# Four array tiles at once for the scores and the triangular products of a chunked delta-rule attention

## Chip, cores and metric

One core of a Trainium2 chip runs the whole program. The metric is the device time of one execution in microseconds (us); less is better. Engines: TensorE (PE, its weight loads PEld), VectorE (DVE), ScalarE (ACT), GpSimd (POOL), and the DMA queues, fed by SyncE (SP).

## The reference

A delta-rule attention over 4 batches x 8 heads, 768 steps, head size 48, then two dense layers with a gate over 3072 tokens of 384 features:

```python
for t in range(S):                                   # S = 768, state is (B, H, 48, 48)
    y[:, :, t] = einsum('bhd,bhde->bhe', q[:, :, t], state)
    v_old = einsum('bhde,bhd->bhe', state, kt)       # kt: normed key of step t
    state = state + bt * einsum('bhd,bhe->bhde', kt, vt - v_old)
x = y as (3072, 384)
x = maximum(maximum(x @ w1, x @ w2), x @ w3) @ w_out  # 768 wide
h = x @ w_in ; out = maximum(0.01 * h, h) @ w_out2    # 2048 wide
```

## The kernel before

The attention is worked in 12 chunks of 64 steps. A chunk's 32 pairs of batch and head are held as 16 "units" u, each with two heads: head 0 on partitions 0 to 63, head 1 on 64 to 127 (keys and queries, whose rows are the head's 48 features, lie the other way round). All attention matmuls are plain fp32, and the trace has two records, here called passes, for each of them. The dense layers use a three-matmul split in fp32r on the full 128 x 128 array (`mm3`, tiles `p` and `acc`, later `z`).

`stage2(c)` is the serial part of chunk c:

- scores and state product, tile `pk` (L240 to L250): a unit's key block is the weight (48 x 64) and [q | state] of 112 columns streams. It is done in four quarters of four units; in each, one matmul uses array rows 64 up and columns 0 to 63 (L245), the other rows 0 up and columns 64 to 127 (L246): two tiles of the array. DVE then subtracts the state part from `v` (L247, 128 x 192) and masks the scores into `W` (L214 in `masked`, twice 64 x 256).
- three triangular products in 32 x 32 blocks (`product`, L255 to L276, matmul L259), each in two halves hf of eight units: `pu` = T x v on the top 32 rows of each head, copied to `W` by ACT (L265); `pv` = GO x pu, subtracted from the low rows of `v` by DVE (L270); `pw` = T x v on the low rows, copied by ACT (L275). `pu` uses the tiles (row, column) (0,0) and (64,64), `pv` (0,32) and (64,96), `pw` (32,32) and (96,96): two tiles each.
- output `py` and state update `psu`; the output goes by DMA (`x<-st`) into the tile `x` that the first dense layer reads.

`stage1` (grams `pg`, and a solve of 31 steps on DVE, L183 and L191) prepares later pairs of chunks, and `moe1` is the first dense layer. `steps` merges these generators by weights: for chunk c, n units of dense work (9, 17, 22, then 24) are laid between the pieces of `stage2(c)` and half a `stage1`. What comes out is only a starting order: a scheduler with a timeline of its own then orders each engine's instructions, and pushes a matmul back whose PSUM buffer is not free. All small products share one ring of three PSUM buffers (tag `pa`, L82). Each engine works through its order without overtaking a waiting instruction.

Of the kernel before, what the change touches and what calls it, by code (L numbers as in the profile page):

```python
# [27 lines left out]
def kernel(  # L28
# [201 lines left out]
    def stage2(c):  # L230
# [8 lines left out]
        if c:  # L239
            for qt in range(4):  # L240
                us = slice(qt * 4, qt * 4 + 4)
                pk = pm.tile([128, 4, C + D], F32, tag="pa", name="pk")
                for j in range(4):
                    u = qt * 4 + j
                    nc.tensor.matmul(pk[0:64, j], kt[64:112, u], W[64:112, 0, u])  # L245
                    nc.tensor.matmul(pk[64:128, j], kt[0:48, u], W[0:48, 1, u])  # L246
                nc.vector.tensor_tensor(v[:, us], v[:, us], pk[:, :, cU], op=ALU.subtract)  # L247
# [7 lines left out]
        def product(name, hf, rows, outs, lhs, rhs):  # L255
            p = pm.tile([128, 8, C], F32, tag="pa", name=name)
            for j in range(8):
                for (s2, r), (_, o) in zip(rows, outs):
                    nc.tensor.matmul(p[o, j, 0:D], lhs[r, par, hf * 8 + j], rhs(s2, r, hf * 8 + j))  # L259
            return p  # L260

        for hf in range(2):
            p = product("pu", hf, tops, tops, T, lambda s2, r, u: v[r, u])
            for s2, r in tops:
                nc.scalar.activation(W[r, s2, hs[hf], cU], p[r, :, 0:D], AF.Copy)  # L265
            yield YU
        for hf in range(2):
            p = product("pv", hf, tops, lows, GO, lambda s2, r, u: W[r, s2, u, cU])
# [2 lines left out]
            yield YU
        for hf in range(2):
            p = product("pw", hf, lows, lows, T, lambda s2, r, u: v[r, u])
            for s2, r in lows:
                nc.scalar.activation(W[r, s2, hs[hf], cU], p[r, :, 0:D], AF.Copy)  # L275
            yield YU  # L276
# [379 lines left out]
```

## Time and profile before

| | us |
|---|---|
| median of 3 runs (lowest, highest) | 974.67 (974.33, 975.55) |
| profiled execution, device time | 976.32 |
| its span, first to last instruction | 974.5 |
| PE busy | 911.3 |
| DVE busy | 630.2 |
| ACT busy | 360.1 |

The span falls into a start (to 75.9 us, chunk 0 and the first solve), chunks 1 to 11 mixed with the first dense layer (75.9 to about 513), and the rest of the dense layers (to the end), in which no attention is left. Matmul ends are modelled and overlap, so the cadence of matmuls is read from the starts of rows, not from their durations.

### The profile page before, as it was taken

The numbers are of one execution on the slowest core, as the hardware profiler recorded it, in microseconds if no ns is written. First come the engines' busy times: TensorE is split into PE (matmuls) and PEld (weight loads), VectorE is DVE, ScalarE is ACT, GpSimd is POOL, SyncE is SP. The second block draws the span as 40 slices with busy tenths as digits, with TensorE's granted clock in tenths as the row PEclk, the third lists the DMA queues.
The fourth block names the chain that finished last, engine by engine and source line by source line (L and its number), as shares of the span: only waits on it lengthen the run. The fifth ranks groups of instructions, "written<-read, shape, count | busy, mean of one in ns | idle before, by whom it ended". The sixth has DMA issues, their size and how long they took to land.

```text
span 974.5 us, 19985 instructions
## 1 busy us (share of the span) xinstructions
PE 911.3 (94%) x8417; PEld 744.2 (76%) x8417; DVE 630.2 (65%) x1314; ACT 360.1 (37%) x702; POOL 12.8 (1%) x15
## 2 busy tenths in 40 slices
PE   5158999899989999999999999999999999999998
PEld 4157887678778877887877888888888888888886
DVE  4999988984984896598345836734753574444443
ACT  5432256324233232421324426635432342232332
POOL 3000000000000000000000000000000000000000
PEclk7555999999999999999999999999999999999999
DMA  9124334221250322303016504300300010000111
GB/s 258 65 90 147 107 115 123 80 60 34 75 139 18 91 83 58 76 27 85 1 35 202 170 1 146 114 1 4 126 1 1 1 49 1 0 1 33 44 54 65
DMA packets 56344, 67.83 MB, mean 70 GB/s; under 512 B 26048, under 2 KB 40000, under 8 KB 56256
## 3 DMA queue, kind: packets, MB, share of 16 engines
q1 hardware_dynamic: 56256, 66.57, 23.2%
q8 instruction: 66, 1.08, 0.5%
q14 instruction: 22, 0.18, 0.1%
HBM read 47.68 MB, written 9.44 MB: 59 GB/s over the span
## 4 chain that ended last, share of the span: by engine, by line
PE 78%; DVE 11%; DMA 4%; SPq 3%; issue 2%; ACT 1%; DVEq 0%; ACTq 0%
PE acc L331 9%; PE acc L333 9%; PE acc L332 9%; PE p L331 7%; PE z L333 7%; PE z L332 7%; PE z L331 7%; PE p L332 7%; PE p L333 6%; DVE X L191 2%; DVE tmp L183 2%; PE pv L259 2%; PE pw L259 2%; PE pk L245 2%; PE pu L259 1%
## 5 line engine op out<-in xcount | busy, mean ns | idle before, releaser
L331 PE MATMUL p<-x,w1s 128*128 128x512 f32 (+1 forms) x351 | 140.3, 400 | 10.7 <-DMA x<-st 7.6
L429 DVE TENSOR_TENSOR g<-z,g 128x512 f32<-128x512 f32 x96 | 66.1, 689 | 107.3 <-ACT g L428 107.2
L332 PE MATMUL p<-x,w1s 128*128 128x512 f32 (+1 forms) x351 | 135.2, 385 | 0.0
L333 PE MATMUL p<-x,w1s 128*128 128x512 f32 (+1 forms) x351 | 134.7, 384 | 0.0
L428 ACT ACTIVATE g<-z 128x512 f32<-128x512 f32 x96 | 57.2, 597 | 155.4 <-PE z L333 155.3
L332 PE MATMUL acc<-gs,w2g 128*128 128x512 f32 x288 | 113.5, 394 | 0.0
L333 PE MATMUL z<-x,w2g 128*128 128x512 f32 x288 | 113.3, 394 | 0.0
L333 PE MATMUL acc<-gs,w2g 128*128 128x512 f32 x288 | 113.3, 393 | 0.0
L332 PE MATMUL z<-x,w2g 128*128 128x512 f32 x288 | 113.3, 393 | 0.0
L331 PE MATMUL z<-x,w2g 128*128 128x512 f32 x288 | 113.3, 393 | 0.0
L331 PE MATMUL acc<-gs,w2g 128*128 128x512 f32 x288 | 109.7, 394 | 0.0
L48 DVE TENSOR_TENSOR gs<-g,gs 128x512 fp32r<-128x512 f32 x96 | 66.2, 689 | 40.5 <-ACT gs L47 39.1
L365 DVE TENSOR_TENSOR a<-p,a 128x512 f32<-128x512 f32 (+1 forms) x78 | 50.5, 647 | 61.5 <-PE p L333 46.5
L331 PEld LDWEIGHTS p<-x,w1s 128*128 128x128 f32 x351 | 67.9, 193 | 28.6 <-DMA x<-st 7.3
L47 ACT ACTIVATE gs<-g 128x512 fp32r<-128x512 f32 x96 | 60.4, 631 | 64.0 <-DVE g L429 63.7
L333 PEld LDWEIGHTS p<-x,w1s 128*128 128x128 f32 x351 | 68.2, 194 | 12.3
L332 PEld LDWEIGHTS p<-x,w1s 128*128 128x128 f32 x351 | 68.3, 195 | 11.3
L191 DVE TENSOR_TENSOR X<-X,tmp 128x31 f32<-128x31 f32 (+15 forms) x186 | 63.4, 341 | 5.1
L183 DVE TENSOR_TENSOR tmp<-A,X 128x31 f32<-128x31 f32 (+15 forms) x186 | 63.4, 341 | 5.0
L47 ACT ACTIVATE h<-a 128x512 fp32r<-128x512 f32 (+1 forms) x37 | 22.5, 608 | 114.6 <-DVE a L365 114.3
L331 PEld LDWEIGHTS z<-x,w2g 128*128 128x128 f32 x288 | 54.2, 188 | 12.6
L331 PEld LDWEIGHTS acc<-gs,w2g 128*128 128x128 f32 x288 | 54.1, 188 | 12.6
(107 smaller groups left out, 1627.3 us busy)
## 6 DMA issues: line engine op xcount, KB each, us to landing
x<-st SPq DMA_DIRECT2D x72, 96.0 KB, 2.5
kt<-ktr SPq DMA_DIRECT2D x12, 512.0 KB, 3.4
cv<-wi SPq DMA_DIRECT2D x16, 384.0 KB, 3.8
cv<-wo SPq DMA_DIRECT2D x16, 384.0 KB, 3.1
rx<-w SPq DMA_DIRECT2D x15, 384.0 KB, 5.6
v<-vro SPq DMA_DIRECT2D x12, 384.0 KB, 3.4
x_scratch<-xo SPq DMA_DIRECT2D x18, 256.0 KB, 2.5
xr<-x_scratch SPq DMA_DIRECT2D x12, 384.0 KB, 3.8
```

Source lines behind the costliest of these rows:

```text
L47: nc.scalar.activation(hi, src, AF.Copy)
L48: eng.tensor_tensor(lo, src, hi.bitcast(F32), op=ALU.subtract)
L183: eng.tensor_tensor(tv, A[:, k : k + 1, k + 1 : 32].to_broadcast([128, w, m]), X[:, a : a + w, k : k + 1].to_broadcast([128, w, m]), op=AL ...
L191: eng.tensor_tensor(X[:, a : a + w, k + 1 : 32], X[:, a : a + w, k + 1 : 32], tv, op=ALU.subtract)
L245: nc.tensor.matmul(pk[0:64, j], kt[64:112, u], W[64:112, 0, u])
L259: nc.tensor.matmul(p[o, j, 0:D], lhs[r, par, hf * 8 + j], rhs(s2, r, hf * 8 + j))
L331: nc.tensor.matmul(ps, whi, xhi, start=first, stop=False)
L332: nc.tensor.matmul(ps, whi, xlo, start=False, stop=False)
L333: nc.tensor.matmul(ps, wlo, xhi, start=False, stop=last)
L365: nc.vector.tensor_tensor(a, p, a, op=ALU.max)
L428: nc.scalar.activation(gg, z, AF.Copy, scale=0.01)
L429: nc.vector.tensor_tensor(gg, z, gg, op=ALU.max)
```

## The change

Quarters of `pk` are taken in pairs: for each unit of the first quarter and its fellow of the second, four matmuls on four tiles, the second quarter's two heads exchanged in the output's partitions (head 0 on 64 to 127). Its subtraction then takes two DVE instructions of 64 partitions in place of one of 128, and `masked` reads from the other half. Of the products, half 0 of `pv` and half 1 of `pu` are issued in turn (tiles in columns 0, 32, 64 and 96), and half 0 of `pw` and half 1 of `pv`; `pu` half 0 and `pw` half 1 stand alone. The dense units for chunks 2 and 3 go from 17 and 22 to 15 and 18.

```diff
-    def masked(W, i, us, p):
-        r = slice(64 * i, 64 * i + 64)
+    def masked(W, i, us, p, e=0):
+        r, o = (slice(64 * n, 64 * n + 64) for n in (i, i ^ e))
...
-        nc.vector.tensor_tensor(W[r, i, us, cP], p[r], mk, op=ALU.mult)
+        nc.vector.tensor_tensor(W[r, i, us, cP], p[o], mk, op=ALU.mult)
...
-            for qt in range(4):
+            for qt in range(0, 4, 2):
+                pk = [pm.tile([128, 4, C + D], F32, tag="pa", name="pk") for _ in range(2)]
+                for j in range(4):
+                    for e in range(2):
+                        u = (qt + e) * 4 + j
+                        o = [slice(64 * (i ^ e), 64 * (i ^ e) + 64) for i in range(2)]
+                        nc.tensor.matmul(pk[e][o[0], j], kt[64:112, u], W[64:112, 0, u])
+                        nc.tensor.matmul(pk[e][o[1], j], kt[0:48, u], W[0:48, 1, u])
                 us = slice(qt * 4, qt * 4 + 4)
...
+                nc.vector.tensor_tensor(v[:, us], v[:, us], pk[0][:, :, cU], op=ALU.subtract)
                 for i in range(2):
...
+                    masked(W, i, us, pk[0][:, :, cP])
+                us = slice(qt * 4 + 4, qt * 4 + 8)
+                for i in range(2):
+                    r, o = slice(64 * i, 64 * i + 64), slice(64 - 64 * i, 128 - 64 * i)
+                    nc.vector.tensor_tensor(v[r, us], v[r, us], pk[1][o, :, cU], op=ALU.subtract)
+                    masked(W, i, us, pk[1][:, :, cP], 1)
+                yield 2 * 970
...
+        def products(*gs):
+            ps = [pm.tile([128, 8, C], F32, tag="pa", name=g[0]) for g in gs]
             for j in range(8):
+                for p, (_, hf, rows, outs, lhs, rhs) in zip(ps, gs):
+                    for (s2, r), (_, o) in zip(rows, outs):
+                        u = hf * 8 + j
+                        nc.tensor.matmul(p[o, j, 0:D], lhs[r, par, u], rhs(s2, r, u))
+            return ps
...
+        keep(0, tops, products(pu(0))[0])
+        yield YU
+        p = products(pv(0), pu(1))
+        less(0, p[0])
+        keep(1, tops, p[1])
+        yield 2 * YU
+        p = products(pw(0), pv(1))
+        less(1, p[1])
+        keep(0, lows, p[0])
+        yield 2 * YU
+        keep(1, lows, products(pw(1))[0])
...
-            n = {1: 9, 2: 17, 3: 22}.get(c, 24)
+            n = {1: 9, 2: 15, 3: 18}.get(c, 24)
```

(`keep` is the ACT copy of L265 and L275, `less` the DVE subtraction of L270.) What the scheduler makes of it on PE, at three places:

PE, the products of chunk 11, before (`pu`, `pv`: 32 x 32 products; `p`: dense matmuls):

```order
L259 MATMUL pu<-v_5397,Tc 32x48 x16
L333 MATMUL p<-x,w1s 128x512
L331 MATMUL p<-x,w1s 128x512
L259 MATMUL pu<-v_5397,Tc 32x48 x16
L259 MATMUL pv<-W_70,GO 32x48
```

PE, the same place in the changed program, from the first `pv` on:

```order
L270 MATMUL pv<-W_70,GO 32x48
L270 MATMUL pu<-v_5380,Tc 32x48
L270 MATMUL pv<-W_70,GO 32x48
L270 MATMUL pu<-v_5380,Tc 32x48
L270 MATMUL pv<-W_70,GO 32x48 x2
L270 MATMUL pu<-v_5380,Tc 32x48 x2
L270 MATMUL pv<-W_70,GO 32x48 x2
L270 MATMUL pu<-v_5380,Tc 32x48 x2
```

The two halves, which stood one after the other, now stand two by two in turn. In chunks 1 to 11 all 11 pairs `pv`/`pu` stand so; of the pairs `pw`/`pv` those of chunks 2, 4, and 6 to 11, while in chunks 1, 3 and 5 they stand wholly or mostly in blocks.

PE, scores of chunk 3 before (the number after `pk_` tells the PSUM buffer of a quarter):

```order
L245 MATMUL pk_1886<-W1_70,kt3_281 64x112
L246 MATMUL pk_1886<-W1_70,kt3_281 64x112
L245 MATMUL pk_1916<-W1_70,kt3_281 64x112
L246 MATMUL pk_1916<-W1_70,kt3_281 64x112
L245 MATMUL pk_1916<-W1_70,kt3_281 64x112
```

PE, in the changed program, chunk 3 (`pk_1879` is the first quarter of a pair, `pk_1880` its fellow):

```order
L247 MATMUL pk_1879<-W1_70,kt3_281 64x112
L248 MATMUL pk_1879<-W1_70,kt3_281 64x112
L247 MATMUL pk_1880<-W1_70,kt3_281 64x112
L248 MATMUL pk_1880<-W1_70,kt3_281 64x112
L247 MATMUL pk_1879<-W1_70,kt3_281 64x112
L248 MATMUL pk_1879<-W1_70,kt3_281 64x112
```

PE, in the changed program, chunk 4, the same two quarters:

```order
L247 MATMUL pk_2323<-W0_69,kt4_1234 64x112
L248 MATMUL pk_2323<-W0_69,kt4_1234 64x112
L247 MATMUL pk_2323<-W0_69,kt4_1234 64x112
L248 MATMUL pk_2323<-W0_69,kt4_1234 64x112
L247 MATMUL pk_2324<-W0_69,kt4_1234 64x112
L248 MATMUL pk_2324<-W0_69,kt4_1234 64x112
```

In chunk 3 the two quarters alternate as the code has them. In chunk 4 all eight matmuls of one quarter stand ahead of the other's eight. Over the kernel the full alternation is there for one pair of quarters in each of chunks 1, 3, 5, 7, 9 and 11 (6 of 22 pairs, in some with a few matmuls in blocks); at 8 other places a quarter follows directly behind one on the other two tiles; the rest have dense work or grams between.

PE, from the second half of the products to `py` in chunk 5, before (`acc`: dense matmuls):

```order
L331 MATMUL acc_2702<-h,wo1s 128x512
L259 MATMUL pw<-v_2347,Tc 32x48 x16
L332 MATMUL acc_2700<-h,wo1s 128x512
L333 MATMUL acc_2700<-h,wo1s 128x512
L332 MATMUL acc_2701<-h,wo1s 128x512
L333 MATMUL acc_2701<-h,wo1s 128x512
L332 MATMUL acc_2702<-h,wo1s 128x512
L333 MATMUL acc_2702<-h,wo1s 128x512
L259 MATMUL pw<-v_2347,Tc 32x48 x16
L287 MATMUL py<-W_70 64x64
```

and changed:

```order
L270 MATMUL pv<-W_70,GO 32x48 x2
L270 MATMUL pu<-v_2318,Tc 32x48 x2
L270 MATMUL pw<-v_2318,Tc 32x48
L270 MATMUL pv<-W_70,GO 32x48 x16
L270 MATMUL pw<-v_2318,Tc 32x48 x31
L312 MATMUL py<-W_70 64x64
```

Here no dense matmul is left between the steps. Between the `pk` of chunk 5 and that of chunk 6 stand 22 dense matmuls in place of 63, and in chunk 4 194 in place of 153. To the first dense `z`, the dense matmuls enter the small ones 78 times in place of 93 (runs of small matmuls with dense ones ahead).

## Rows read from the trace of the kernel before

**Rows 1.** The page, parts 1, 2 and 4: busy time, share and count of PE and DVE; the granted PE clock in 40 slices (tenths); the chain that ended last, by engine.

```profile
PE 911.3 (94%) x8417; PEld 744.2 (76%) x8417; DVE 630.2 (65%) x1314; ACT 360.1 (37%) x702; POOL 12.8 (1%) x15
PEclk7555999999999999999999999999999999999999
PE 78%; DVE 11%; DMA 4%; SPq 3%; issue 2%; ACT 1%; DVEq 0%; ACTq 0%
```

**Rows 2.** Busy time by stretch: stretch, its length, then for PE, PEld, DVE, ACT, POOL busy us (instructions), granted clock, DMA share, GB/s. The stretches are chunks 1, 2, 3, 5, 6, 7, and most of 9.

```profile
75.90:109.90 34.00, 33.27 (x465) 29.61 (x465) 32.52 (x85) 10.67 (x22) 0.00 (x0) 0.68 0.37 114
109.90:159.30 49.40, 47.87 (x672) 39.75 (x673) 43.02 (x100) 25.80 (x57) 0.00 (x0) 1.00 0.48 132
159.30:189.40 30.10, 26.30 (x451) 21.48 (x446) 27.05 (x67) 12.35 (x26) 0.95 (x1) 1.00 0.29 87
...
244.20:271.90 27.70, 27.70 (x457) 22.48 (x451) 26.33 (x66) 8.51 (x17) 0.00 (x0) 1.00 0.39 103
271.90:326.60 54.70, 52.18 (x651) 41.79 (x651) 33.14 (x70) 19.03 (x43) 0.95 (x1) 0.97 0.23 59
326.60:358.20 31.60, 31.24 (x473) 25.20 (x467) 29.44 (x75) 9.14 (x18) 0.00 (x0) 1.00 0.33 95
...
410.00:440.00 30.00, 30.00 (x419) 24.37 (x418) 28.10 (x68) 7.70 (x15) 0.00 (x0) 1.00 0.21 51
```

**Rows 3.** PE's waits between 75 and 550 us: who waited for whom, us in total, times, longest.

```profile
PE p L331 <- DMA x<-st: 7.6, 5, 2.7
PE p L331 <- DVE a L365: 2.0, 3, 1.3
PE psu L311 <- DVE st L292: 1.7, 2, 1.3
PE pu L259 <- DVE W L214: 1.6, 2, 1.0
```

**Rows 4.** Groups of instructions by line and form: busy us, mean ns of one | idle before. PE counts are passes, two for each matmul.

```profile
L245 PE MATMUL pk<-W,kt 48*64 48x112 f32 x352 | 43.6, 272 | 1.1 <-PE psu L312 0.8 <-DVE W L316 0.3
L259 PE MATMUL pv<-W,GO 32*32 32x48 f32 x768 | 25.2, 212 | 0.7 <-ACT W L265 0.6
L247 DVE TENSOR_TENSOR v<-v,pk 128x192 f32<-128x192 f32 x44 | 15.4, 349 | 5.4 <-PE pk L246 4.7
```

**Rows 5.** Timeline of PE in chunk 5, `pk`: start us, duration, engine, line, operation.

```profile
250.13 0.26 PE L245 MATMUL pk<-W,kt 48*64 48x112 f32 x1
250.14 0.26 PE L246 MATMUL pk<-W,kt 48*64 48x112 f32 x1
...
252.05 0.26 PE L245 MATMUL pk<-W,kt 48*64 48x112 f32 x1
252.06 0.26 PE L246 MATMUL pk<-W,kt 48*64 48x112 f32 x1
```

**Rows 6.** Timeline of PE in chunk 5: dense matmuls, both halves of `pu` (64 passes merged in one row), dense matmuls.

```profile
254.31 0.39 PE L332 MATMUL p<-x,w1s 128*128 128x512 f32 x1
254.54 0.40 PE L333 MATMUL p<-x,w1s 128*128 128x512 f32 x1
254.87 1.55 PE L259 MATMUL pu<-v,Tc 32*32 32x48 f32 x64
256.35 0.50 PE L331 MATMUL p<-x,w1s 128*128 128x512 f32 x1
256.68 0.40 PE L332 MATMUL p<-x,w1s 128*128 128x512 f32 x1
```

**Rows 7.** Timeline of PE in chunk 3, where half 1 of `pu` is followed directly by half 0 of `pv`, in the program's order all `pu` first.

```profile
173.86 0.23 PE L259 MATMUL pv<-W,GO 32*32 32x48 f32 x2
173.89 0.21 PE L259 MATMUL pu<-v,Tc 32*32 32x48 f32 x2
173.93 0.20 PE L259 MATMUL pv<-W,GO 32*32 32x48 f32 x1
...
173.97 0.20 PE L259 MATMUL pv<-W,GO 32*32 32x48 f32 x1
173.98 0.20 PE L259 MATMUL pu<-v,Tc 32*32 32x48 f32 x1
173.98 0.20 PE L259 MATMUL pv<-W,GO 32*32 32x48 f32 x1
173.99 0.20 PE L259 MATMUL pu<-v,Tc 32*32 32x48 f32 x1
174.02 0.24 PE L259 MATMUL pv<-W,GO 32*32 32x48 f32 x3
```

**Rows 8.** Timeline of PE in chunk 1, where half 0 of `pw` follows half 1 of `pv`.

```profile
98.93 0.23 PE L259 MATMUL pw<-v,Tc 32*32 32x48 f32 x1
98.93 0.20 PE L259 MATMUL pv<-W,GO 32*32 32x48 f32 x1
98.94 0.23 PE L259 MATMUL pw<-v,Tc 32*32 32x48 f32 x1
98.97 0.21 PE L259 MATMUL pv<-W,GO 32*32 32x48 f32 x2
```

**Rows 9.** Timeline of all engines in chunk 0: the evacuations between the products.

```profile
60.93 0.98 ACT L265 ACTIVATE W<-pu 32x384 f32<-32x384 f32 x2
61.46 1.75 PE L259 MATMUL pv<-W,GO 32*32 32x48 f32 x27 [0.60 <-ACT W L265]
63.76 1.14 DVE L270 TENSOR_TENSOR v<-v,pv 32x384 f32<-32x384 f32 x2
```

**Rows 10.** Busy time and granted clock by stretch, columns as in rows 2, around the first rise of the clock; and the timeline row of the wait at the start of chunk 6.

```profile
75.90:94.00 18.10, 18.10 (x187) 15.68 (x187) 17.44 (x50) 6.08 (x13) 0.00 (x0) 0.50 0.58 181
94.00:97.60 3.60, 3.60 (x20) 3.34 (x17) 3.37 (x8) 0.66 (x2) 0.00 (x0) 0.50 0.02 5
97.60:101.00 3.40, 3.40 (x78) 3.08 (x78) 3.17 (x9) 0.97 (x2) 0.00 (x0) 0.96 0.00 0
275.40:278.80 3.40, 3.38 (x16) 2.36 (x18) 2.20 (x6) 0.00 (x0) 0.00 (x0) 0.51 0.45 116
275.42 0.77 PE L331 MATMUL p<-x,w1s 128*128 128x512 f32 x1 [2.30 <-DMA x<-st]
```

More of the change, by code (lines that the diff above doesn't have):

```diff
@@ L239, in stage2 @@
         if c:
-            for qt in range(4):
-                us = slice(qt * 4, qt * 4 + 4)
[L242 to L247, printed above, removed]
-                for i in range(2):
-                    masked(W, i, us, pk[:, :, cP])
-                yield 970
+            for qt in range(0, 4, 2):
[6 more added lines that the diff above has]
+                        nc.tensor.matmul(pk[e][o[1], j], kt[0:48, u], W[0:48, 1, u])
+                us = slice(qt * 4, qt * 4 + 4)
+                nc.vector.tensor_tensor(v[:, us], v[:, us], pk[0][:, :, cU], op=ALU.subtract)
+                for i in range(2):
+                    masked(W, i, us, pk[0][:, :, cP])
[5 more added lines that the diff above has]
+                yield 2 * 970
         T, GO = tcs[c - par], go[c - par]
@@ L253, in stage2, with pu, pv, pw @@
         lows = ((0, slice(32, 64)), (1, slice(96, 128)))
-        def product(name, hf, rows, outs, lhs, rhs):
-            p = pm.tile([128, 8, C], F32, tag="pa", name=name)
+        def products(*gs):
+            ps = [pm.tile([128, 8, C], F32, tag="pa", name=g[0]) for g in gs]
             for j in range(8):
[L258 to L264, printed above, removed]
+                for p, (_, hf, rows, outs, lhs, rhs) in zip(ps, gs):
[3 more added lines that the diff above has]
+            return ps
+        def pu(hf):
+            return "pu", hf, tops, tops, T, lambda s2, r, u: v[r, u]
+        def pv(hf):
+            return "pv", hf, tops, lows, GO, lambda s2, r, u: W[r, s2, u, cU]
+        def pw(hf):
+            return "pw", hf, lows, lows, T, lambda s2, r, u: v[r, u]
+        def keep(hf, rows, p):
+            for s2, r in rows:
                 nc.scalar.activation(W[r, s2, hs[hf], cU], p[r, :, 0:D], AF.Copy)
-            yield YU
-        for hf in range(2):
-            p = product("pv", hf, tops, lows, GO, lambda s2, r, u: W[r, s2, u, cU])
+        def less(hf, p):
             for s2, r in lows:
                 nc.vector.tensor_tensor(v[r, hs[hf]], v[r, hs[hf]], p[r, :, 0:D], op=ALU.subtract)
[L271 to L276, printed above, removed]
+        keep(0, tops, products(pu(0))[0])
[9 more added lines that the diff above has]
+        keep(1, lows, products(pw(1))[0])
+        yield YU
         if par == 0:
```

## The prediction, made before the changed kernel was run

> **What bounds the kernel now.** The page's shares come first: PE is busy 94% of the span, DVE 65%, and the chain that ended last is 78% PE [rows 1]. The change touches only `stage2`, so the next view is busy time by chunk. Chunks 1, 2 and 3 leave PE idle 0.7, 1.5 and 3.8 us of 34.0, 49.4 and 30.1 us, chunk 5 leaves it none, chunk 7 0.4 of 31.6 [rows 2]: PE sets the pace. But DVE is close behind, at 96%, 87% and 90% in chunks 1 to 3 and at 95%, 93% and 94% in chunks 5, 7 and 9, in which the solve lies; in chunk 6 it is at 61%. The list of waits says what PE does wait for: the largest item is the output's DMA into `x`, 7.6 us in five waits; waits for DVE are 1 to 2 us each [rows 3]. So PE work that goes away in chunks 1 to 11 shortens the time as long as DVE and the chain of steps inside a chunk follow.
>
> **What the change is worth on PE.** *Slots.* Two `pk` passes start 10 ns apart on their two tiles, and the next two 96 ns later: from 250.13 to 252.05 there are 20 such steps [rows 5]. I call one a slot. The 64 passes of both halves of `pu` take 1.55 us with 0.20 us for the last, so 43 ns for a slot of two [rows 6].
>
> *Do four tiles share a slot?* In chunk 3, where `pv` follows `pu` on two other tiles, four passes start at 173.97, 173.98, 173.98 and 173.99, and the next at 174.02: four in a slot of 43 ns, on four column groups and two row groups [rows 7]. Where `pw` follows `pv`, with the same column groups and other rows, passes of both start together too, at 98.93 and 98.94 [rows 8]. So four tiles work at the speed of two, for 32 x 32 tiles at least. The 64 x 64 tiles of `pk` are shown by no row; between no gain (96 ns for two passes) and all of it (96 ns for four) I take all of it, by the nearest rows.
>
> The Trainium skill ("TensorE: Matmul & The Clock Gate", Part 3, The mechanism) says that matmuls start and end strictly in program order and only weight loads are pulled ahead. As each fp32 matmul is two passes on one tile, the second tile would then start only behind the first's second pass, and four tiles would be worth no more than two; the trace disagrees, since `pv` passes start at 173.86, ahead of `pu` passes at 173.89 that stand before them in the program.
>
> *How much of it the new order has.* Products: `pv` with `pu` in turn in 11 chunks saves 16 slots each, 176; `pw` with `pv` about 16 in chunks 2, 4, 6, 7, 8, 15 in chunks 9 to 11, and some 17 in chunks 1, 3 and 5 together, where the blocks overlap only at their seam: 142. Together 318 x 43 ns = 13.6 us, less some 0.7 us of such seams that the kernel has already (five, three slots each, as in rows 7): **12.9 us**. `pk`: the saving of all 22 pairs would be 8 slots each, 16.8 us. Only six pairs alternate: five at 8 x 96 ns and that of chunk 1, at half the clock [rows 10], at 8 x 191 ns, in all 5.3 us; eight seams at three slots give 2.3 us, less 0.3 us for the blocks: **7.3 us**. The rest stays as it was, since the second quarter's buffer is not free in time.
>
> *Fewer changes of shape.* Going from a dense matmul to `pu` takes 0.33 us from start to start instead of 0.23, the first dense one starts 0.13 us behind the last `pu` slot instead of 0.04, and the next 0.33 later instead of 0.23 [rows 6]: 0.29 us for one insertion. 15 fewer are 4.3 us; eight more changes among small shapes cost some 0.1 us each: **3.5 us**.
>
> **What it costs.** *DVE.* 22 more subtractions: half the partitions, the same 192 elements, so the 349 ns of the group [rows 4], 7.7 us in chunks 1 to 11. That the reads cross partition halves has no row: between nothing and another 0.35 us for each of the 88 instructions that do so, four to a pair of quarters (31 us of DVE), I take nothing. In even chunks it lies beside idle DVE time; in chunks 1 to 3, 5, 7 and 9, where DVE has 1.4 to 6.4 us left, it and the shorter PE work meet. I take **2 us** given back; the other bound is rival A.
>
> *Chunk 5.* 22 dense matmuls in place of 63 leave the steps bare: `pw` waits for both subtractions (1.14 us [rows 9]) and then for the next two, with the DVE queue ahead of them some 2 us each: **4 us**. The work is not lost, it stands in chunk 4.
>
> *Chunk 0.* Nothing dense exists yet. Before, half 1 of `pu` covered ACT's 0.98 us, and still 0.60 us of a wait was left [rows 9]; now half 0 of `pv` stands before it. One ACT pair and one DVE pair (0.98 and 1.14 us) come on the path to the first `x`: **2 us**.
>
> *The clock.* It stands at 0.50, the 1.2 GHz level, until 97.6 us, with PE busy all the time, and is 0.96 in the next stretch, behind 15 dense matmuls in a row [rows 10]. The new order has 18 in a row one step earlier, where 9 were. If the clock rises there, 4 to 5 us of work run at 2.4 GHz: **2 us** gained, between 0 and 2.5.
>
> *Waits for `x`.* At chunk 8's start dense work of the old block is left as cover. Of the 7.6 us [rows 3] I take **1 us** off, between 0 and 3. The smaller counts of dense units change nothing by themselves: the dense matmuls ahead of chunk 4 are as many as before.
>
> **Sum.** 12.9 + 7.3 + 3.5 + 2 + 1 - 2 - 4 - 2 = 18.7 us. The profiled execution has a span of 974.5 us and a device time of 976.3 us; the median of the runs is 974.67 us, 0.2% below, and I take the sum from the median: **956 us**. A difference of under 0.2% (2 us) can't be told from no change here.
>
> **Rivals.**
>
> A. *DVE becomes the bound.* In chunks 1 to 3 and 5, 7, 9 nothing is gained, for DVE was at 87 to 96% and gets more [rows 2]. What is left is chunks 4, 6, 8, 10 and 11, each some 32 product slots and a seam or more of `pk`, 8 us together, and 2 us of insertions, less the 2 us of chunk 0: 967 us. For it speaks how near DVE is; against, that the even chunks have DVE idle and the order moves solve work there. The Trainium skill ("TensorEngine Tiling (Array Packing)", PSUM Bottleneck) warns of just this, that tiling speeds TensorE and not the evacuation; so far the trace bears it out in the DVE shares alone.
>
> B. *The 64 x 64 tiles do not share.* The 7.3 us of `pk` are gone: 963 us. Against it only the 32 x 32 rows speak.
>
> C. *No four tiles at all*, by program order: 20.2 us gone, 976 us, no change. Rows 7 and 8 speak against it.
>
> D. *Slower: the bare chain.* A product step left without cover costs about 2 us, as in chunk 5. There are three steps in each of 11 chunks; the new order shows cover of 9 to 18 dense matmuls (2 to 4 us at 0.23 us) at nearly all others. If evacuation takes longer than that behind a full DVE queue, nine more bare steps eat the gain; at fifteen the time is 986 us. Idle stretches can also cost the clock: behind the 2.30 us wait for `x` it stood at 0.51 for 3.4 us [rows 10], some 1.7 us lost each time.
>
> E. *More is gained.* PE's waits, of which the four largest items make 12.9 us [rows 3], vanish for the most part: some 10 us more, 946 us.
>
> **How the numbers follow.** The forecast (950 to 962 us) has 0.55, E 0.10, A 0.15, B 0.08, C 0.04, D 0.08. The range 945 to 970 takes in E, A and B and leaves out C and D and the tails of the others. Faster 0.88, same 0.04 (C), slower 0.08 (D).
>
> **What would show it.** Products right: rows where `pv` and `pu` passes start four to 43 ns, and PE busy down by some 20 us. `pk` right: in chunk 3 four `pk` passes to 96 ns; wrong if the alternation takes 96 ns for two. Costs: PE idle of some 4 us in chunk 5, the first `p` some 2 us later than 75.9 us, the clock's rise before 97.6 us. A is right if DVE's share in chunks 1 to 3, 7 and 9 reaches 97% and PE's waits there name DVE; D, if PE waits for `W` (ACT) and `v` (DVE) in most chunks. The stretch behind the attention should keep its length. The prediction is wrong above all if PE's waits grow by more than 10 us.

## The result, and the profile after

The changed kernel takes 985.36 us (median; 982.76 to 988.6) against 975.11 us for the kernel before on the same chip: ratio 1.010, 95% interval 1.0065 to 1.0134. It is slower by 1.0%, where 956 us was forecast. The profiled execution has a span of 986.6 us and a time of 988.6 us.

The page, parts 1, 2 and 4 [rows 1]:

```profile
PE 908.4 (92%) x8417; PEld 738.2 (75%) x8417; DVE 633.1 (64%) x1336; ACT 359.0 (36%) x702; POOL 12.8 (1%) x15
PEclk7556999899978999998999999999999999999999
PE 73%; DVE 17%; DMA 3%; SPq 3%; issue 2%; ACT 2%; DVEq 0%; ACTq 0%
```

PE is busy only 2.9 us less, the clock row has three 8s and a 7 behind the start where before it had only 9s, and DVE's part of the chain went from 11% to 17%. Busy time by stretch, chunks 1 to 11 and what lies behind them (columns as in rows 2):

```profile
79.00:109.00 30.00, 27.34 (x462) 23.67 (x461) 28.82 (x75) 9.18 (x20) 0.00 (x0) 0.77 0.41 120
109.00:156.40 47.40, 44.90 (x673) 37.68 (x672) 43.16 (x102) 26.17 (x60) 0.00 (x0) 1.00 0.50 140
156.40:186.00 29.60, 26.06 (x440) 20.90 (x441) 26.02 (x65) 11.63 (x24) 0.95 (x1) 0.94 0.24 78
186.00:254.40 68.40, 65.83 (x716) 52.83 (x713) 42.91 (x95) 21.01 (x46) 0.95 (x1) 0.93 0.18 46
254.40:279.20 24.80, 21.02 (x418) 17.75 (x413) 21.70 (x55) 7.37 (x15) 0.00 (x0) 0.79 0.45 124
279.20:333.00 53.80, 45.96 (x615) 36.82 (x615) 34.35 (x77) 17.85 (x41) 0.95 (x1) 0.87 0.21 55
333.00:367.60 34.60, 34.38 (x489) 27.20 (x485) 32.84 (x84) 8.00 (x15) 0.00 (x0) 1.00 0.27 67
...
547.20:986.60 439.40, 435.06 (x1882) 353.28 (x1880) 229.49 (x391) 166.58 (x291) 0.00 (x0) 1.00 0.14 46
```

Chunks 1 to 3 take 107.0 us where before they took 112.0 (first `pk` to first `pk`, 77.4 to 189.4), with the same 291 dense matmuls. Chunks 4 and 5 take 93.2 instead of 82.7 (189.4 to 272.1), also with the same number, 216; but 194 of them stand in chunk 4 and 22 in chunk 5. The stretch from the first `z` to the end is 439.4 us in both. PE's waits between 75 and 550 us [rows 3]:

```profile
PE p L356 <- DMA x<-st: 12.3, 10, 2.7
PE pk L247 <- DVE W L214: 5.7, 4, 3.0
PE pw L270 <- DVE v L288: 3.4, 3, 2.3
PE pu L270 <- DVE Tc L196: 3.2, 2, 2.8
```

Waits that name DVE sum to 16.3 us over all items of the list, 6.9 before; all waits sum to 31.0 us, 17.2 before. Then the clock: five places of the changed kernel at which it fell, each with the stretch ahead of it (same columns).

```profile
186.00:189.40 3.40, 1.99 (x42) 1.55 (x37) 2.82 (x5) 0.00 (x0) 0.00 (x0) 1.00 0.84 180
189.40:199.60 10.20, 9.04 (x68) 6.91 (x70) 6.31 (x18) 2.24 (x6) 0.00 (x0) 0.50 0.47 113
264.50:267.90 3.40, 1.48 (x67) 0.94 (x65) 3.15 (x11) 2.60 (x5) 0.00 (x0) 1.00 0.42 154
267.90:278.10 10.20, 9.58 (x200) 8.95 (x202) 7.66 (x18) 2.70 (x6) 0.00 (x0) 0.50 0.19 68
284.00:288.40 4.40, 1.50 (x34) 1.17 (x29) 4.19 (x13) 2.25 (x6) 0.00 (x0) 1.00 0.74 165
288.40:295.20 6.80, 6.03 (x50) 4.74 (x52) 6.49 (x19) 0.60 (x1) 0.00 (x0) 0.50 0.34 109
298.00:302.00 4.00, 1.84 (x9) 1.18 (x7) 3.66 (x11) 0.00 (x0) 0.00 (x0) 1.00 0.00 0
302.00:308.80 6.80, 6.16 (x43) 5.11 (x44) 2.42 (x4) 2.08 (x4) 0.95 (x1) 0.50 0.01 2
448.50:452.20 3.70, 1.02 (x17) 0.84 (x17) 3.65 (x8) 0.63 (x1) 0.00 (x0) 1.00 0.37 89
452.20:459.00 6.80, 6.80 (x35) 4.74 (x37) 3.82 (x10) 0.00 (x0) 0.00 (x0) 0.50 0.60 130
```

With one more of 3.4 us at 168.9 that is 44 us at the 1.2 GHz level behind 100 us, against 3.4 us before [rows 10]. What that costs, in the timeline of PE: dense matmuls start 427 ns apart at half the clock, some 230 ns at 2.4 GHz.

```profile
170.27 0.63 PE L356 MATMUL p<-x,w1s 128*128 128x512 f32 x1
170.69 0.63 PE L357 MATMUL p<-x,w1s 128*128 128x512 f32 x1
...
172.61 0.40 PE L356 MATMUL p<-x,w1s 128*128 128x512 f32 x1
172.84 0.39 PE L357 MATMUL p<-x,w1s 128*128 128x512 f32 x1
```

**The ledger.** From the first `pk` to the end a span divides into three: PE idle; time lost to the half clock (PE's busy time in half-microsecond stretches, times one minus the granted clock); and the rest, PE's work at 2.4 GHz. For before: 19.0 + 11.9 + 866.2 us. All kernels below, as differences to that, in the profiled execution of each ("start": when the first `pk` starts, against 77.4 us):

| kernel | median us | ratio to before (95%) | start | idle | half clock | work |
|---|---|---|---|---|---|---|
| changed kernel | 985.4 | 1.010 (1.0065 to 1.0134) | +1.5 | +14.9 | +14.7 | -19.1 |
| e1 products only | 967.4 | 0.9914 (0.9892 to 0.9936) | +2.0 | -2.5 | +4.0 | -11.0 |
| e2 pairs only | 983.4 | 1.0075 (1.0052 to 1.0098) | -1.8 | +5.8 | +10.0 | -6.3 |
| e3 two tiles | 979.0 | 1.0028 (1.0009 to 1.0048) | +1.8 | +8.8 | +8.3 | -14.0 |
| e4 hold in chunk 5 | 974.0 | 0.998 (0.9957 to 1.0003) | +1.9 | +4.0 | +11.4 | -16.7 |
| e5 filled, 13 places | 990.5 | 1.0145 (1.0116 to 1.0175) | +0.9 | +11.9 | +0.4 | +1.1 |
| e6 two tiles, same order | 991.9 | 1.015 (1.0119 to 1.0181) | +2.9 | +15.1 | +12.3 | -15.3 |
| e7 filled, 7 places | 980.5 | 1.0036 (1.0019 to 1.0053) | +1.8 | +5.8 | +4.7 | -7.2 |
| e8 spread, pairs | 978.4 | 1.0004 (0.998 to 1.0029) | +3.3 | +14.6 | +1.8 | -17.4 |
| e9 spread, single | 977.4 | 1.0008 (0.9989 to 1.0028) | +1.3 | +4.7 | +5.6 | -11.3 |
| e10 holds from 5, pairs | 978.0 | 1.0002 (0.9974 to 1.0031) | +1.5 | +5.4 | +8.1 | -17.1 |
| e11 same, pairs from 4 | 968.9 | 0.9901 (0.9868 to 0.9933) | +1.4 | +7.2 | +5.7 | -19.3 |
| e12 same, single | 974.9 | 0.9977 (0.9952 to 1.0002) | +2.0 | -0.2 | +8.4 | -11.5 |
| e13 short subtractions | 978.1 | 1.0006 (0.9982 to 1.0029) | +0.5 | +13.6 | +10.7 | -18.9 |
| e14 spread late, pairs | 976.1 | 0.9982 (0.9962 to 1.0003) | +0.4 | +7.7 | +11.2 | -21.2 |
| e15 same, pairs from 4 | 977.9 | 1.002 (0.9999 to 1.0042) | +0.4 | +16.9 | +4.5 | -20.9 |
| e16 before, split | 984.1 | 1.0044 (1.0013 to 1.0076) | -0.3 | +1.8 | +9.1 | +0.9 |
| e17 products, pairs from 4 | 978.0 | 1.0 (0.9982 to 1.0019) | +1.4 | +7.3 | +10.1 | -15.1 |
| e18 products, pairs from 6 | 969.0 | 0.9901 (0.9874 to 0.9928) | +1.0 | +2.6 | +2.5 | -14.4 |

The changed kernel did save the work: 19.1 us. Idle time, the half clock and the later start took 31.1 us.

Each row of the ledger is one execution, and its time lies up to some 4 us off the median of its kernel (e16 988.1 against 984.1, e13 982.4 against 978.1, e10 974.2 against 978.0). In chunks 1 to 3, PE's instructions stand in the same order in e1, e11, e12 and e17; these chunks take 109.8, 113.3, 110.8 and 114.3 us there. In the changed kernel, e13, e4 and e10, again of one order there, they take 107.0, 107.2, 110.8 and 106.8. So a few us of idle time or half clock in one row, or of one chunk, can't be told from chance. The work column is steadier: e13 has the changed kernel's PE order and is 0.2 us off it, e16 has that of the kernel before and is 0.9 off.

### The profile page after: what moved, and what is told of

The parts are those of the page before. It is cut to its first block, busy times and chain, and to the rows that moved or that the text cites. A ratio compares the mean times of both kernels' runs of the same rounds, so it can differ in the third digit from the quotient of the medians.

```text
span 986.6 us, 20011 instructions
## 1 busy us (share of the span) xinstructions
PE 908.4 (92%) x8417; PEld 738.2 (75%) x8417; DVE 633.1 (64%) x1336; ACT 359.0 (36%) x702; POOL 12.8 (1%) x15
## 4 chain that ended last, share of the span: by engine, by line
PE 73%; DVE 17%; DMA 3%; SPq 3%; issue 2%; ACT 2%; DVEq 0%; ACTq 0%
PE acc L356 9%; PE acc L357 9%; PE acc L358 9%; PE z L358 7%; PE z L357 7%; PE z L356 7%; PE p L356 6%; PE p L357 6%; PE p L358 6%; DVE tmp L183 3%; DVE X L191 3%; DVE W L214 2%; PE pw L270 2%; DMA x<-st 2%; PE pg L124 1%
## 5 line engine op out<-in xcount | busy, mean ns | idle before, releaser
L356 PE MATMUL p<-x,w1s 128*128 128x512 f32 (+1 forms) x351 | 142.6, 406 | 14.3 <-DMA x<-st 12.3
L357 PE MATMUL p<-x,w1s 128*128 128x512 f32 (+1 forms) x351 | 136.9, 390 | 0.0
L358 PE MATMUL p<-x,w1s 128*128 128x512 f32 (+1 forms) x351 | 136.3, 388 | 0.0
L358 PE MATMUL acc<-gs,w2g 128*128 128x512 f32 x288 | 113.3, 393 | 0.0
L357 PE MATMUL z<-x,w2g 128*128 128x512 f32 x288 | 113.3, 393 | 0.0
L356 PE MATMUL z<-x,w2g 128*128 128x512 f32 x288 | 113.3, 393 | 0.0
L356 PEld LDWEIGHTS p<-x,w1s 128*128 128x128 f32 x351 | 68.6, 196 | 33.9 <-issue 10.2
L358 PEld LDWEIGHTS p<-x,w1s 128*128 128x128 f32 x351 | 69.2, 197 | 13.3
L357 PEld LDWEIGHTS p<-x,w1s 128*128 128x128 f32 x351 | 69.3, 198 | 12.0 <-issue 0.3
```

Source lines behind the costliest of these rows:

```text
L356: nc.tensor.matmul(ps, whi, xhi, start=first, stop=False)
L357: nc.tensor.matmul(ps, whi, xlo, start=False, stop=False)
L358: nc.tensor.matmul(ps, wlo, xhi, start=False, stop=last)
```

## Experiments: which part

Theory O: the new order leaves PE bare at some steps, above all in chunk 5, and the clock falls behind each stop, while the packing is worth what was forecast. Rival Q: the products in turn are what costs. Rival K: the pairs of score quarters are. e1 puts the block of `pk` back, e2 that of the products, both with the old units; e3 keeps the whole change but for the exchange of heads:

```diff
-            n = {1: 9, 2: 15, 3: 18}.get(c, 24)
+            n = {1: 9, 2: 17, 3: 22}.get(c, 24)
```
```diff
-                        o = [slice(64 * (i ^ e), 64 * (i ^ e) + 64) for i in range(2)]
+                        o = [slice(64 * i, 64 * i + 64) for i in range(2)]
```

> Only the products in turn; the score quarters stand as in the kernel before (one buffer, two tiles), and the counts of dense units are the old ones. The order has 86 dense matmuls in chunk 5. Theory O (the order: too few dense matmuls in chunk 5 and a few bare steps stop PE, and the clock falls behind each stop; the packing itself is worth what was predicted): 975.1 - 12.9 - 3.5 + 2 = about 961 us, under 10 us of the attention phase at half clock. Rival Q (the products in turn are the cost: steps that need both halves at once leave PE bare everywhere): 980 us or more. Rival K (the pair of score quarters, its two buffers and six evacuations, is the cost): 961 us too.

> Only the pairs of score quarters; the three products stand as in the kernel before, with the old counts. 77 dense matmuls in chunk 5. Theory O: 975.1 - 7.3 + 2 (22 more subtractions) = about 970 us. Rival K: 980 us or more, with PE waits of 5 us or more at pk for DVE's masked writes of W. Rival Q: 970 us.

> The changed kernel without the exchange of heads: both quarters of a pair still stand in turn in two buffers, but on the same two tiles, and the second quarter has one subtraction on 128 partitions in place of two on 64. The scheduler's order comes out with 81 dense matmuls in chunk 5 in place of 22. Theory O: the packing of pk is lost (7.3 us) but the stops and the low clock of chunks 4 to 6 go: 963 to 968 us. Rival K: the pair is still there: 985 us or more. Rival Q: 985 us or more.

The products alone are 0.9% faster, with their 11.0 us of work saved and 3.5 us lost again: rival Q is out, and this is a kernel that beats both, though at 967 us it stays short of the 961 forecast. The pairs alone are slower (983 us, 970 forecast) although they save 6.3 us of work. That is rival K's time, but the waits of e2 don't name what K named, `pk` waiting for `W`, for which the changed kernel's list has 5.7 us:

```profile
PE p L339 <- DMA x<-st: 9.5, 10, 2.6
PE psu L319 <- DVE st L300: 4.2, 4, 3.4
PE p L339 <- DVE a L373: 3.2, 2, 2.7
```

These waits are for evacuations and for `x`, at many places. Why the order of e2 makes them isn't shown. e3 missed theory O's forecast by 11 us: with 81 dense matmuls in chunk 5 it still has 8.8 us more idle time and 8.3 us of half clock, at other places (around 200 and 378 us). Bare steps in chunk 5 alone do not explain the loss. Nor does added work on DVE: e3 has no more DVE instructions than the kernel before (1314).

**The packing of `pk` by itself.** Each change of the source makes the scheduler order everything anew. In e5, e6, e7, e13 and e16 the order is held: a chain of order-only edges binds every engine to a list of its instructions. (What these edges cost by themselves has no run of its own; e13 counts 20012 instructions, the changed kernel 20011.) e6 is e3's edit on the output tiles, with the two 64-row subtractions kept, in the changed kernel's order:

```diff
-                    r, o = slice(64 * i, 64 * i + 64), slice(64 - 64 * i, 128 - 64 * i)
+                    r = o = slice(64 * i, 64 * i + 64)
```

> The changed kernel with every engine's order held as it is and only the exchange of heads undone: the second quarter of each pair runs on the same two tiles as the first, so its passes follow instead of sharing a slot. All instructions, waits and their order are those of the changed kernel. This prices the packing of pk alone. Theory O: slots of 96 ns are back in the six alternating pairs and eight seams, 5 to 7 us more PE work: 990 to 993 us. Rival N (four 64 x 64 tiles are worth nothing, or what they give is lost in waits): 985 us.

991.9 us, as forecast, but with 3.8 us more work where 5 to 7 were expected: four 64 x 64 tiles do share, and taking that away costs work. In time it is 0.5% in the ratios, with intervals that overlap a little. Chunk 3's `pk` in the changed kernel shows the sharing directly, as the prediction asked, four passes to a slot of some 96 ns:

```profile
156.64 0.26 PE L247 MATMUL pk<-W,kt 48*64 48x112 f32 x1
156.65 0.26 PE L248 MATMUL pk<-W,kt 48*64 48x112 f32 x1
156.66 0.26 PE L247 MATMUL pk<-W,kt 48*64 48x112 f32 x1
156.66 0.26 PE L248 MATMUL pk<-W,kt 48*64 48x112 f32 x1
156.74 0.26 PE L247 MATMUL pk<-W,kt 48*64 48x112 f32 x1
```

## Experiments: stops and clock

e4 holds back dense work for chunk 5; the same edit with other tables makes e8 to e12, e14 and e15:

```diff
+    PIN = {5: (10, 24)}
+    def pinned(g, c):
+        done, (lo, hi) = 0, PIN.get(c, (0, 0))
+        while True:
+            with tc.issue_after(last["pk", c]) if lo <= done < hi else ExitStack():
+                w = next(g, None)
...
-            gens = [(stage2(c), S2, 0, END), (count(mos, n), n, 0, 1)]
+            gens = [(stage2(c), S2, 0, END), (pinned(count(mos, n), c), n, 0, 1)]
```

> The changed kernel with one thing more: the last 14 of the 24 dense units that the program has in chunk 5 may not be issued on PE ahead of chunk 5's first pk matmul. Chunks 0 to 3 keep their order; chunk 4 has 126 dense matmuls in place of 194, chunk 5 72 in place of 22. Theory O: chunks 4 and 5 together lose the 10 us that they are longer than before (93.2 us against 82.7): about 975 us, and no stretch at 0.5 clock between 250 and 310 us. Rivals Q and K: the stops stay, since the steps are the same: within 3 us of the changed kernel's 985.

974.0 us, the number that theory O gave, some 11 us less than the changed kernel. But it did not come where theory O put it. Of the 68 dense matmuls that leave chunk 4, 50 stand in chunk 5 and the rest later. Chunks 4 and 5, then chunk 6, of e4:

```profile
190.20:281.10 90.90, 83.27 (x1103) 66.64 (x1097) 73.03 (x174) 26.05 (x56) 0.95 (x1) 0.91 0.23 59
281.10:325.80 44.70, 43.04 (x613) 33.55 (x613) 25.86 (x57) 19.31 (x44) 0.95 (x1) 0.96 0.31 85
```

Chunks 4 and 5 take 90.9 us with 198 dense matmuls, where the changed kernel took 93.2 with 216: 18 fewer, which are 4.1 us at 0.23 us, so nothing was gained there. Chunk 6 takes 44.7 us in place of 53.8, with two dense matmuls fewer, and chunk 10 41.8 in place of 50.6, with nine fewer. So that the number came out is in part luck. The ledger still has 11.4 us of half clock, now at other places; the forecast that there would be none between 250 and 310 us fell (247.5 to 258, 295 to 299). e5 and e7 keep the order and fill the stops with useless matmuls:

```diff
                 p = pm.tile([128, 2 * TOK], F32, tag="p", name="p", bufs=2)[:, m]
+                for at, k in FILL.get(count_p[0], ()):
+                    put[at] = [nc.tensor.matmul(p, w1s[:, 0, 0, 0], w1s[:, 0, 0, 0 : 2 * n]).ins for _ in range(k)]
+                count_p[0] += 1
```

> The changed kernel with every engine's order held as it is, and 96 matmuls more that compute nothing: 3 to 12 dense ones written into the next p tile (and overwritten there) just ahead of each of 12 places at which PE stood still 0.7 us or more (78.1, 98.6, 111.5, 164.4, 168.2, 188.2, 190.6, 268.3, 281.1, 289.2, 302.6, 374.7 and 452.1 us), in number so that they last about as long as the stop. Theory O with the clock as its part (each stop costs itself and then a stretch at 0.5 clock): the stops stay as long as they are, filled, but most of the 44 us at 0.5 behind 100 us go, worth 12 to 17 us: 968 to 973 us. Rival W (the waits alone cost the time, the clock would be low anyway): 985 to 988 us, since work that nobody needs cannot shorten a wait.

> The filled kernel of the run before with fewer places: fillers only where the next p tile was free (111.5, 188.2, 190.6, 268.3, 281.1, 289.2 and 452.1 us of the changed kernel), since at 168 and 306 us the fillers themselves waited 4.8 and 5.1 us for DVE to free a p tile. Every engine's order is held, DMA issues too. Theory O with the clock as its part, sized by chunks 4 and 10 of that run, which came out 3.8 and 3.4 us shorter than in the changed kernel: 976 to 979 us. If the whole low clock were worth its 17 us: 970. Rival W (waits alone): 985 to 987.

e5 came out at 990.5 us, slower than any theory had it, since two groups of fillers had to wait for a `p` tile, 4.8 and 5.1 us. Its ledger has nearly nothing of the clock's loss (+0.4 us), in part because the clock stood at its full level from the start of chunk 1 to 91.6 us; behind 100 us, 24 us at the 1.2 GHz level are left of 44. The second of the two waits in e5's timeline:

```profile
306.20 0.79 PE L391 MATMUL p<-w1s 128*128 128x512 f32 x1 [5.13 <-DVE a L399]
```

e7, without such places, takes 980.5 us: 0.65% less than the changed kernel in the ratios, by 54 matmuls that compute nothing (forecast 976 to 979). Its ledger against the changed kernel: work +11.9 (the fillers), idle -9.1, half clock -10.0 us. Chunk 10 takes 47.2 us in place of 50.6, with no fall of the clock at its start. Behind 100 us 17 us at the 1.2 GHz level are left. Rival W is out, since the intervals of the two kernels lie apart. One stop grew: chunk 6's first `pu` now waits 5.8 us for `Tc`, the solve on DVE, where the changed kernel waited 2.8.

```profile
PE pu L270 <- DVE Tc L196: 6.2, 2, 5.8
```

## Experiments: DVE's load

Theory L says that DVE's added load causes the stops, theory P that the place of the dense matmuls does. e13 shrinks 22 subtractions of the changed kernel to an element a row, so it leaves out a part of the state product; e16 adds the same 22 to the kernel before, all orders held in both:

```diff
-                    nc.vector.tensor_tensor(v[r, us], v[r, us], pk[1][o, :, cU], op=ALU.subtract)
+                    w = slice(us.start, us.start + 1) if i else us
+                    d = slice(0, 1) if i else slice(0, D)
+                    nc.vector.tensor_tensor(v[r, w, d], v[r, w, d], pk[1][o, : w.stop - w.start, C:][:, :, d], op=ALU.subtract)
```
```diff
-                nc.vector.tensor_tensor(v[:, us], v[:, us], pk[:, :, cU], op=ALU.subtract)
+                if qt % 2 == 0:
+                    nc.vector.tensor_tensor(v[:, us], v[:, us], pk[:, :, cU], op=ALU.subtract)
+                else:
+                    a, b = (
+                        nc.vector.tensor_tensor(v[r, us], v[r, us], pk[r, :, cU], op=ALU.subtract)
+                        for r in (slice(0, 64), slice(64, 128))
+                    )
```

> The changed kernel, every engine's order and the DMA issues held, with the second of the two 64-row subtractions of each pair's second quarter shrunk to one element a row (a part of the state is then not subtracted): 22 instructions of some 0.35 us on DVE shrink to about 0.06, some 6 us less DVE work in chunks 1 to 11, as much as the change had added. Theory L (DVE's added load causes the stops): most of the 6 us come back, and with them clock: 976 to 980 us. Theory P (the place of the dense matmuls causes them): 983 to 986 us.

> The kernel before, every engine's order held, with the subtraction of every second score quarter (128 rows) split into two of 64 rows: 22 instructions more on DVE, the same 7.7 us that the change adds, and nothing else. Theory L (DVE is so near to being the bound that its load alone costs): 3 to 9 us slower than before, 978 to 985 us, with stops of PE in chunks 1, 3, 5, 7, 9. Theory P (DVE's load hides where dense matmuls are well spread): within 2 us of before.

Both came out as theory L said. A shrunk subtraction takes 151 ns in place of 351, not the 0.06 us expected, so 4.4 us of DVE work are taken away and not 6:

```profile
L258 DVE TENSOR_TENSOR v<-v,pk 64x1 f32<-64x1 f32 x22 | 3.3, 151 | 0.4
```

These give 0.95% in the ratios (1.010 to 1.0006; the intervals leave 4 to 15 us), and 7.7 us added cost the kernel before 0.44%, some 4 us (the interval leaves 1 to 7). So DVE's load is a cause; e3, slower without it, shows that it isn't the only one. In e16's profiled execution, which was 4 us above its median, PE is idle only 1.8 us more; 9.1 us are half clock. One place of it is the start of chunk 10, where PE waits for `x`. In the timeline of the kernel before, and in that of e16:

```profile
443.73 0.47 PE L331 MATMUL p<-x,w1s 128*128 128x512 f32 x1 [1.58 <-DMA x<-st]
```
```profile
452.13 0.47 PE L340 MATMUL p<-x,w1s 128*128 128x512 f32 x1 [1.82 <-DMA x<-st]
```

The stretches that end with this wait and those behind it, of the kernel before, then of e16 (columns as in rows 2); PE's instructions are the same in the same order but for passes that start together:

```profile
440.00:443.70 3.70, 2.15 (x48) 1.53 (x46) 3.57 (x9) 0.90 (x2) 0.00 (x0) 1.00 0.37 93
443.70:450.50 6.80, 6.77 (x61) 4.92 (x62) 5.92 (x17) 0.00 (x0) 0.00 (x0) 1.00 0.73 160
```
```profile
448.40:452.10 3.70, 1.92 (x47) 1.33 (x45) 3.57 (x9) 0.67 (x2) 0.00 (x0) 1.00 0.36 84
452.10:458.90 6.80, 6.77 (x37) 4.96 (x38) 5.30 (x15) 0.00 (x0) 0.00 (x0) 0.63 0.64 143
```

Behind a stop that is 0.24 us longer the clock fell to the 1.2 GHz level for 6.8 us, from 453.9 us on; in the 6.8 us from the wait's end 37 passes stand instead of 61. That the 0.24 us made the fall isn't shown, and the length of a stop alone does not decide. One wait for `x` in chunk 2, in the changed kernel, in e4 with the same PE order up to there, and in e11:

```profile
111.52 0.35 PE L356 MATMUL p<-x,w1s 128*128 128x256 f32 x1 [1.57 <-DMA x<-st]
111.60 0.55 PE L357 MATMUL p<-x,w1s 128*128 128x256 f32 x1 [2.11 <-DMA x<-st]
111.93 0.35 PE L372 MATMUL p<-x,w1s 128*128 128x256 f32 x1 [1.53 <-DMA x<-st]
```

With the first no fall came, with the second and third 6.8 us at the 1.2 GHz level each. The Trainium skill ("TensorEngine Tiling (Array Packing)", PSUM Bottleneck) warns that tiling speeds up TensorE and not the evacuation, which may then bound. e13 and e16 agree in that DVE's evacuations cost time, though DVE is at 64% of the span and was at 88% in chunks 3 and 5 of the changed kernel.

## Experiments: looking for an order in which the saving shows

e8 and e9 (with single quarters, as before) use the holds of e4 with this table and these units:

```diff
+    PIN = {2: (0, 2), 3: (6, 18), 4: (0, 6), 5: (10, 24), 6: (0, 6), 7: (10, 24), 8: (0, 6), 9: (10, 24), 10: (0, 6)}
-            n = {1: 9, 2: 15, 3: 18}.get(c, 24)
+            n = {1: 7, 2: 17, 3: 18}.get(c, 24)
```

> The changed kernel (pairs and products in turn) with its dense units spread by hand: units 7, 17 and 18 for chunks 1 to 3 instead of 9, 15 and 18; the last 12 to 14 units of chunks 3, 5, 7 and 9 may not be issued ahead of that chunk's first pk, and the first 6 (2) of chunks 4, 6, 8 and 10 (2), which belong to the block before, neither, so that they stand where PE waits for x. Dense matmuls in chunks 1 to 11: 57, 126, 81, 128, 88, 131, 85, 134, 82, 126, 153. Theory O: with cover at every step the saved PE work of 18.6 us shows: 955 to 962 us, under 12 us at 0.5 clock behind 100 us. Rival K (the pair itself costs): 970 or more, and slower than the next kernel.

> The same holds and units with single score quarters as in the kernel before, and the products in turn. Dense matmuls in chunks 1 to 11: 57, 153, 54, 150, 66, 108, 99, 117, 99, 122, 166. Theory O: some 5 us slower than the spread kernel with pairs (the packing of pk), 962 to 967 us. Rival K: faster than the one with pairs, about 960.

e8 missed by 16 us or more, e9 by 10, and the two are not told apart. From chunk 4 on e8 does what was hoped: chunks 4 to 10 take 281 us (200.0 to 481.1) for 774 dense matmuls, before 299 us (189.4 to 488.8) for 784. But 27 more dense matmuls stand behind the first `z` (445.6 us to the end in place of 439.4), and chunk 2 takes 57.6 us, with a stop of 6.2 us in which a `pg` waits for DVE's `st`, and the clock at 0.77:

```profile
108.30:165.90 57.60, 44.33 (x646) 37.80 (x641) 48.41 (x111) 27.44 (x63) 0.95 (x1) 0.77 0.46 125
...
245.20:278.60 33.40, 31.79 (x479) 25.20 (x475) 31.70 (x82) 8.01 (x15) 0.00 (x0) 1.00 0.25 69
278.60:326.10 47.50, 47.50 (x645) 38.56 (x647) 29.60 (x64) 18.83 (x44) 0.95 (x1) 0.96 0.28 79
```

In chunk 5 DVE is at 95%, as in the kernel before [rows 2], still short of the 97% of rival A's sign. e10 to e12 take the units 9, 15, 18 again and hold nothing before chunk 5; e11 and e12 choose by chunk between the two blocks of `pk` (`range(4, 12)` and none):

```diff
+    PIN = {5: (10, 24), 6: (0, 6), 7: (10, 24), 8: (0, 6), 9: (10, 24), 10: (0, 6)}
+    PAIR = range(4, 12)
-        if c:
+        if c in PAIR:
```

> The changed kernel with the old order kept in chunks 1 to 3 (units 9, 15, 18, nothing held there) and the holds of the spread kernel from chunk 5 on: the last 14 units of chunks 5, 7, 9 not ahead of that chunk's first pk, the first 6 of chunks 6, 8, 10 neither. Dense matmuls in chunks 1 to 11: 75, 160, 56, 126, 63, 108, 99, 117, 99, 131, 157. Theory B (what counts is how PE's dense work and DVE's work are shared out between neighbouring chunks; the spread kernel lost 18 us in chunks 1 to 3, where DVE has the conversions and solves, and won 15 us from chunk 4 on): both good halves come together, 958 to 964 us. Theory K (the pair costs): 970 or more.

> As the kernel before this one, but chunks 1 to 3 take single score quarters (as before) and only chunks 4 to 11 take pairs. Dense matmuls: 75, 165, 51, 101, 88, 112, 104, 116, 100, 122, 157. Theory B: 958 to 964 us, 4 us less than the next kernel, whose pk passes do not share slots. Theory K: slower than the next kernel.

> The same units and holds with single score quarters in all chunks, products in turn. Dense matmuls: 75, 165, 51, 102, 87, 108, 99, 117, 99, 122, 166, so nearly those of the kernel with pairs from chunk 4: the pair of these two prices the pairing in chunks 4 to 11. Theory B: 962 to 968 us, as the products alone (967) or a little less. Theory K: faster than with pairs.

All three missed theory B: e10 by 14 us, e11 by 5, e12 by 7. e11 and e12 differ by the pairs in chunks 4 to 11 and have nearly the same spread: pairs win 6 us (0.9901 against 0.9977), theory K is out there. In the ledger, though, e11's 7.8 us of further work saved stand beside 7.4 us more idle time. e10 with pairs everywhere is 9 us slower than e11. Its profile shows no price of pairs in chunks 1 to 3: these take 106.8 us in e10's (78.9 to 185.7) and 113.3 in e11's (78.9 to 192.2), for 291 dense matmuls each. e10 loses behind, in chunks 4 and 5 (90.4 us against 85.2), with some 17 us at half the clock between 229 and 254 us, and 4.1 us in chunks 6 to 11. But the two profiled executions are only 2.8 us apart, so where the 9 us of the medians lie isn't shown.

e14 (pairs everywhere) and e15 (`PAIR` from 4) add `3: (6, 18), 4: (0, 6)` to that table; e17 and e18 (`PAIR` from 4 and from 6) have no holds and the old units:

> The changed kernel with its own units (9, 15, 18) and the holds of the spread kernel from chunk 3 on (last 12 units of chunk 3; first 6 of chunks 4, 6, 8, 10; last 14 of chunks 5, 7, 9). Dense matmuls: 75, 135, 54, 153, 63, 108, 99, 117, 99, 117, 171. By the ledger (work 18 us less, stops and clock of chunks 1 and 2 as in the changed kernel, behind chunk 4 as in the spread kernel): 957 to 964 us. If the order of chunks 2 and 3 bares DVE's chain there again: 970 or more.

> The same holds with single quarters in chunks 1 to 3 and pairs in chunks 4 to 11. Dense matmuls: 75, 135, 54, 128, 88, 131, 85, 133, 83, 131, 175; from chunk 4 on the order is that of the spread kernel. By the ledger: chunks 1 to 3 113 us less 6 for 27 dense matmuls that move to chunk 4, the rest as in the spread kernel: 962 to 966 us. If pairs in chunks 1 to 3 were the cause of the loss: faster than the kernel before this one; if not: 3 to 6 us slower.

> Products in turn, pairs of score quarters in chunks 4 to 11 only, the old units (9, 17, 22, 24) and no holds, so chunks 1 to 3 are those of the products alone. Dense matmuls: 75, 165, 51, 134, 82, 108, 99, 117, 99, 117, 171. If the pairs' packing shows (4 to 6 us): 961 to 964 us. If DVE's load takes it: 967 or more.

> The same with pairs in chunks 6 to 11 only. Dense matmuls: 75, 165, 51, 125, 86, 127, 94, 116, 91, 140, 148, so chunks 1 to 5 are those of the products alone (967 us). If the packing shows (3 to 4 us for 12 pairs): 963 to 965 us; if DVE's load takes it: 967 or more.

None of the four came to the time at which the saving shows; e14, e17 and e18 lie in the other arm of their forecasts, and e15 misses its 962 to 966 us. Stops and clock took 5 to 21 us each time, at new places. e15 against e14 (1.002 and 0.9982, intervals that touch) gives pairs in chunks 1 to 3 no loss. e18 is level with e1: chunks 6 to 11, where it has pairs, take 253.6 us and 253.5 in e1, with 716 dense matmuls each. e17 is 0.9% slower than e1 in the ratios, some 8 us, while it saves 4 us more work; of the 11.2 us between the two profiled executions 4.5 lie in chunks 1 to 3, where PE's order is the same. The best kernels here are e1, e11 and e18, 0.9% to 1% faster than before and by their intervals not told apart.

## Why the prediction was wrong

**Right: the work.** *Slots* and *do four tiles share* hold. Of 23.7 us forecast for PE's work (12.9 products, 7.3 `pk`, 3.5 insertions) 19.1 are there; the products give 11.0 by themselves (e1, with the insertions of its order), `pk` 6.3 (e2, likewise) or 3.8 (e6 against the changed kernel), half of its term. Rivals B and C are out. That reads across partition halves cost nothing was right as well:

```profile
L256 DVE TENSOR_TENSOR v<-v,pk 64x192 f32<-64x192 f32 x44 | 15.4, 351 | 2.8 <-PE pk L248 2.2
L214 DVE TENSOR_TENSOR W<-pk,mask 64x256 f32<-64x256 f32 x88 | 36.7, 417 | 0.4
```

**Right: single costs.** The first `p` of chunk 1 starts at 78.10 us in place of 75.88 (2 us forecast). PE idles 3.8 us in chunk 5 (4 forecast), but only 2.5 us of them are the wait that was named, `pw` for DVE's `v`; the rest is luck. The clock rises at 93.8 us in place of 97.6.

**Wrong: the clock, +2 forecast, -14.7 in the ledger.** This is the step that failed most. The earlier rise was there: up to 100 us the half clock took 6.0 us in place of 10.2. Behind it the half clock took 20.5 us in place of 1.6, and for that the sum had no term. The prediction had priced a fall of the clock from rows 10 (1.7 us), but left the falls to rival D with 0.08. The idle time of chunk 5 was counted; the 10.2 us at half clock behind it were not. That the clock itself costs time, and not only the stops, e7 shows.

**Wrong: DVE, 2 us given back.** The 7.7 us were counted right and put beside idle DVE time by shares of chunks. Held orders give DVE's load a price of some 9 us for 4.4 (e13) and of some 4 us for 7.7 (e16); in the single executions of the ledger the larger part of both is half clock. Waits that name DVE grew by 9.4 us. Rival A's test, a share of 97%, was not met (96% in chunk 1, 95% in 7); so A's sign for DVE as the limit was too coarse.

**Wrong: waits for `x`, 1 us off forecast.** They went from 7.6 us in five waits to 12.3 in ten; `x` comes from `st`, which DVE writes.

**Wrong: the sum.** It took stops and clock of the kernel before as given but for chunk 5, chunk 0 and the waits for `x`. They belong to an order, and the order was new throughout: PE's idle time grew by 14.9 us, its listed waits by 13.8, more than the 10 us by which the prediction called itself wrong. D, with 986 us, came nearest. Of its signs, PE waiting for ACT's `W` isn't in the list of waits and `pw` waiting for DVE's `v` stands there three times, not in most chunks; the clock that it named beside them is what came.

**Open.** Which stops are followed by a fall was read, not forecast: 1.57 us at 111.5 us in the changed kernel was followed by none, 1.53 us at that wait in e11 by one. How the loss divides between DVE's added load and the new places of the dense matmuls isn't shown either. Nor was an order found that keeps all the work saved without new stops, so it isn't shown that 956 us can be had.

## What to carry to other kernels

Where a scheduler orders the program anew, price a change in three accounts, work, stops and half-clock time, and compare them by neighbouring chunks; work saved on the busiest engine need not be time saved when another engine stands at 90% of the same chunk (e1 kept some 8 of its 11 us, the changed kernel none of its 19). To learn what a part is worth, hold every engine's order and change that part alone; kernels that were ordered anew gave the same pairs anything from 6 us won to 8 us lost. Count the dense work of each chunk in the new order, and look where a change of it shows: 50 dense matmuls more in chunk 5 came with 11 us less, and chunks 6 and 10 had them, not 4 and 5. Profile more than one execution before a few us of one chunk are explained; here one and the same order took 109.8 to 114.3 us for chunks 1 to 3.
